# A later routing chain and spread lower parts in the first expert mixture

## The chip, the cores and the metric

The kernel runs on one core of one Trainium2 chip. The metric is the device time of one execution in microseconds. Three executions of the kernel before took 829.95, 829.97 and 831.6 us; the median is 829.97 us.

A core has five engines that run side by side, each through a queue of its own in order: TensorE (PE in the profile; its weight loads are PEld), VectorE (DVE), ScalarE (ACT), GpSimd (POOL) and SyncE (SP), which issues the plain DMAs. They wait for each other on semaphores only.

## The reference

Three stages follow one another. The first is a linear-attention recurrence with complex decay over 4 batches, 8 heads, 768 steps and 48 channels; its result is 3072 tokens of 384 values. The second is a mixture of experts with a fixed capacity:

```python
logits = x @ w_gate                      # 3072 x 8
order = np.argsort(-logits.flatten())
for idx in order:                        # best pairs first
    tok, e = int(idx) // E, int(idx) % E
    if assigned[tok] >= 0 or counts[e] >= cap: continue
    assigned[tok] = e; counts[e] += 1    # cap = 3072 / 8 = 384
for e in range(E):
    mask = assigned == e
    out[mask] = np.maximum(x[mask] @ w1[e], 0.0) @ w2[e]   # 384 -> 1024 -> 384
```

Every expert gets exactly 384 tokens, but which ones depends on all the others. The third stage is a mixture without capacity: a token whose score is positive goes to its best expert, the result is scaled by a softmax weight and added to the token; all other tokens pass unchanged.

## The kernel before

The attention takes the first 298 us of the profiled execution. The change starts behind it, in `moe1` (line 1230), the capacity mixture; the last mixture (`moe2_round`, line 1323) follows it.

**Routing.** `route` (line 794) finds, in round p, the expert that fills up next and its 384 tokens. It looks for the threshold of the scores in four digits of six bits each. One digit is: 0/1 rows `R` on DVE (line 833), twelve products `hist` on PE that count them (line 849), `need` and `junk` on DVE (lines 854, 855), one small product `ce` on PE (line 859), `bp` on DVE (line 861), and then `A`, `C` and `R` of the next digit. After the fourth digit DVE makes `es` (line 885, the expert's number), `MT` (its members), and the keys of the next round (`prelude`, line 214: `lgm`, `best`, `eq`, `kx`, `dg` and so on). `slots` (line 902) turns the members into row numbers: two products `pp`, a chain on DVE that ends in `L` (line 939) and `R2` (line 931), twelve products `pi` (line 944), and on DVE `odd`, `x` and `ids` (lines 949 to 956). The round of expert p + 1 runs during the products of expert p.

**Products.** Every float32 product is made of three: each operand is split into a high part (`hi`, ACT, line 980) and a lower part (`lo` = raw - hi, line 981), and high by high, high by low and low by high are added (PASSES). Layer 1 (line 1022) has 8 half blocks of 9 products `psh` each; after each, ACT makes the high part of `hT` (line 1035) and DVE the lower part (line 1036), and two PSUM tiles take turns, so the products of half block f + 2 wait for the lower part of f. Layer 2 (line 1068) has 72 products `psy`. The gathered rows `xg` of the next expert are transposed (`pst`, line 1018) inside layer 2 and split into `xT` (lines 989, 990). `ffn1_out` (line 1100) and `route2` (line 1115) then send an expert's result to the last mixture: products `px` and `pp`, some thirty small DVE operations, and six indirect DMAs on POOL (line 116).

**Weights.** An expert has eight tiles of raw weights (`weights`, line 967), four for each layer, in four buffers: a load into a buffer waits until the lower part has read what was there. `fetch_w` (line 992) loads the first four as soon as `es` is known. `fetch_x` (line 1002) issues three indirect DMAs on POOL that gather `xg`, and the other four loads.

**What sets the order.** `layer1` and `layer2` call `tick` (line 1240) twice per half block: 16 times in layer 1 and 16 in layer 2. A routing generator that yields the number n goes on n ticks later; COUNT, SUMS, NEXT, RANKS and ROWS (line 60) are these numbers, for round 0, 1, 2 and so on. PE's order in this stage is the order of the code, held by added dependencies (`pe`, line 100). On the other engines a scheduler decides at build time; once built, each queue is fixed.

## Time and profile before

| what | value |
|---|---|
| median of three executions | 829.97 us |
| the profiled execution's own time | 835.9 us |
| its span, first to last instruction | 834.1 us |
| attention | 0 to about 298 us |
| routing of the first expert and wait for its rows | 298 to 332.5 us |
| experts 0 to 5 of the capacity mixture | 332.5 to 597.3 us |
| expert 6, with no routing left | 597.3 to 626.7 us |
| expert 7 and the last mixture | 626.7 to 834.1 us |

An expert is counted from its first `psh` product to the next expert's first. "Busy" of an engine is the union of its instructions in a stretch. "idle before" is the time for which an engine stood still in front of an instruction, and behind the arrow stands what released it. PEclk is the granted share of TensorE's full clock: 1.00 is 2.4 GHz, 0.50 is 1.2 GHz.

### The profile page before, as it was taken

The numbers are of one execution on the slowest core, as the hardware profiler recorded it, in microseconds if no ns is written. First come the engines' busy times: TensorE is split into PE (matmuls) and PEld (weight loads), VectorE is DVE, ScalarE is ACT, GpSimd is POOL, SyncE is SP. The second block draws the span as 40 slices with busy tenths as digits, with TensorE's granted clock in tenths as the row PEclk, the third lists the DMA queues.
The fourth block names the chain that finished last, engine by engine and source line by source line (L and its number), as shares of the span: only waits on it lengthen the run. The fifth ranks groups of instructions, "written<-read, shape, count | busy, mean of one in ns | idle before, by whom it ended". The sixth has DMA issues, their size and how long they took to land.

```text
span 834.1 us, 14172 instructions
## 1 busy us (share of the span) xinstructions
PE 700.2 (84%) x5162; PEld 642.7 (77%) x5162; DVE 529.6 (63%) x1438; ACT 389.9 (47%) x680; POOL 266.5 (32%) x190
## 2 busy tenths in 40 slices
PE   1578879889999952888888979698899989999992
PEld 1468778778989942677777869598799888999992
DVE  8859779788746557766667676858434455454450
ACT  5775678677745303135242332324323445455540
POOL 1000544634511002010404031313322467677750
PEclk9669899999999975889898999999899999999997
DMA  9996354643211005233333232326402466566620
GB/s 192 222 263 130 67 129 105 138 96 81 54 39 39 20 29 180 72 109 94 108 102 96 84 116 92 117 74 205 141 30 63 137 208 217 177 208 219 225 97 12
DMA packets 183775, 99.80 MB, mean 120 GB/s; under 512 B 130899, under 2 KB 180937, under 8 KB 183696
## 3 DMA queue, kind: packets, MB, share of 16 engines
q1 hardware_dynamic: 178000, 86.79, 38.7%
q0 software_dynamic: 5696, 12.02, 4.3%
q8 instruction: 42, 0.69, 0.3%
q14 instruction: 37, 0.30, 0.1%
HBM read 82.03 MB, written 22.27 MB: 125 GB/s over the span
## 4 chain that ended last, share of the span: by engine, by line
PE 42%; DVE 17%; DMA 15%; issue 9%; ACT 9%; POOL 4%; SPq 1%; POOLq 0%; DVEq 0%; ACTq 0%
PE psy L109 11%; DMA raw<-in_moe_w_dram 11%; PE psh L109 8%; DVE lo L981 4%; PE py L109 4%; PE pa L109 3%; PE pt L112 3%; PE f L436 3%; PE hist L109 3%; PE px L109 3%; ACT hi L980 2%; PE st L109 2%; DVE hT L1036 1%; PE pst L112 1%; DMA xs<-x,ix 1%
## 5 line engine op out<-in xcount | busy, mean ns | idle before, releaser
L109 PE MATMUL psh<-xT,hi 128*128 128x384 f32 (+1 forms) x720 | 142.5, 330 | 21.4 <-DVE hT L1036 19.8
L980 ACT CAST hi<-raw 128x768 fp32r<-128x768 f32 x128 | 106.7, 835 | 104.3 <-DMA raw<-in_moe_w_dram 81.2
L109 PEld LDWEIGHTS psh<-xT,hi 128*128 128x128 f32 x720 | 116.6, 194 | 27.8 <-DVE hT L1036 24.2
L109 PE MATMUL psy<-hT,hi 128*128 128x384 f32 x384 | 105.4, 357 | 0.0
L981 DVE TENSOR_TENSOR lo<-raw,hi 128x768 fp32r<-128x768 f32 x82 | 86.0, 1067 | 30.5 <-ACT hi L980 30.2
L981 POOL TENSOR_TENSOR lo<-raw,hi 128x768 fp32r<-128x768 f32 x46 | 85.1, 1871 | 29.2 <-ACT hi L980 28.7
L116 POOL DMA_INDIRECT xs<-x,ix x24 | 28.0, 1167 | 199.5 <-issue 109.1
L1036 DVE SCALAR_TENSOR_TENSOR hT<-psh,hT 128x384 fp32r<-128x384 f32 (+1 forms) x120 | 59.1, 499 | 45.8 <-ACT hT L1035 44.8
L1035 ACT ACTIVATE hT<-psh 128x384 fp32r<-128x384 f32 (+1 forms) x120 | 53.1, 446 | 73.9 <-PE psh L109 69.4
L109 PE MATMUL psh<-xT,lo 128*128 128x384 f32 (+1 forms) x360 | 76.2, 320 | 0.0
L109 PE MATMUL psy<-hi,hT 128*128 128x384 f32 x272 | 74.9, 346 | 0.0
L109 PEld LDWEIGHTS psy<-hT,hi 128*128 128x128 f32 x384 | 72.8, 200 | 1.1 <-issue 0.2
L109 PE MATMUL psy<-hT,lo 128*128 128x384 f32 x192 | 69.8, 364 | 0.0
L989 ACT CAST xT<-pst 128x384 fp32r<-128x384 f32 (+1 forms) x47 | 19.0, 442 | 101.5 <-PE pst L112 101.5
L109 PEld LDWEIGHTS psh<-xT,lo 128*128 128x128 f32 x360 | 61.0, 193 | 0.0
L109 PE MATMUL pa<-qT,kT 96*128 96x128 f32 x384 | 52.9, 284 | 1.7 <-ACT kT L501 1.7
L109 PEld LDWEIGHTS pa<-qT,kT 96*128 96x128 f32 x384 | 49.2, 200 | 2.5 <-ACT kT L501 1.8
L1006 POOL DMA_INDIRECT xg<-xd,ids x24 | 26.5, 1104 | 75.6 <-PE ce L109 41.5
L109 PEld LDWEIGHTS psy<-hi,hT 128*128 128x128 f32 x272 | 49.0, 192 | 0.0
L990 DVE TENSOR_TENSOR xT<-pst,xT 128x384 fp32r<-128x384 f32 (+1 forms) x47 | 22.3, 499 | 39.6 <-ACT xT L989 39.5
L109 PE MATMUL px<-iw,yT 128*128 128x104 f32 (+1 forms) x336 | 45.7, 281 | 0.7 <-ACT yT L552 0.7
L109 PE MATMUL psy<-lo,hT 128*128 128x384 f32 x136 | 46.0, 338 | 0.0
(342 smaller groups left out, 1478.9 us busy)
## 6 DMA issues: line engine op xcount, KB each, us to landing
raw<-in_moe_w_dram SPq DMA_DIRECT2D x128, 384.0 KB, 4.0
xs<-zt SPq DMA_DIRECT2D x8, 579.0 KB, 7.0
re<-in_a_re_dram SPq DMA_DIRECT2D x24, 192.0 KB, 3.7
im<-in_a_im_dram SPq DMA_DIRECT2D x24, 192.0 KB, 3.7
q<-in_q_dram SPq DMA_DIRECT2D x24, 192.0 KB, 3.6
k<-in_k_dram SPq DMA_DIRECT2D x24, 192.0 KB, 3.8
vp<-in_v_dram SPq DMA_DIRECT2D x24, 192.0 KB, 3.3
xd<-xo SPq DMA_DIRECT2D x24, 192.0 KB, 1.9
```

The source lines that it names most:

```text
L109: return pe(nc.tensor.matmul(*a, **kw))
L112: return pe(nc.tensor.transpose(*a))
L116: st = nc.gpsimd.indirect_dma_start(out=dst, out_offset=bass.IndirectOffsetOnAxis(ap=idx, axis=0), in_=src, in_offset=None, bounds_check=b ...
L436: nc.tensor.matmul(f, lhsT=m, rhs=x, start=(j == 0), stop=(j == len(mm) - 1))
L980: nc.scalar.copy(out=hi, in_=raw)
L981: st = (V if g in shared else nc.gpsimd).tensor_tensor(out=lo, in0=raw, in1=hi.bitcast(F32), op=ALU.subtract)
L989: nc.scalar.copy(out=xT[0][:, c, :], in_=ps)
L990: V.tensor_tensor(out=xT[1][:, c, :], in0=ps, in1=xT[0][:, c, :].bitcast(F32), op=ALU.subtract)
L1006: st = nc.gpsimd.indirect_dma_start(out=xg[:, j, :], out_offset=None, in_=xd, in_offset=bass.IndirectOffsetOnAxis(ap=ids[:, j:j + 1], axis=0))
L1035: nc.scalar.activation(out=hT[0][:, f, :], in_=ps, func=ACTF.Relu)
L1036: V.scalar_tensor_tensor(out=hT[1][:, f, :], in0=ps, scalar=0.0, in1=hT[0][:, f, :].bitcast(F32), op0=ALU.max, op1=ALU.subtract)
```

## The change

The numbers that set the ticks change. A pause REST of 5 ticks comes between the end of a round and the next round's keys; COUNT goes from 14 to 16 and then 10, RANKS from 4 to 2, ROWS from 8 to 5, and the transposes go from tick 11 to tick 13 of layer 2. Weight tiles beyond the first four are no longer fetched when the rows are, but one at a time; their lower parts are put in a list, `lows`, and every third tick takes one from it. For round 1 the first three digits have one-tick pauses, and they run, with the transposes of expert 0's rows, in seven ticks ahead of expert 0's first product. The instructions and their number on each engine stay the same, and so does the order on SP and POOL.

```diff
-    COUNT, SUMS, NEXT, RANKS, ROWS = (1, 14), (1, 3), (1, 2), (3, 2, 4), (10, 10, 8)
-    START, TURN, AHEAD = 4, 11, 4
+    REST, COUNT, NEXT, SUMS, RANKS, ROWS = 5, (16, 10), 2, 3, 2, 5
+    START = 7
+    TURN, AHEAD, LOW = 13, 4, 3
...
-        def pause(v):
-            return 1 if p == 0 else v[min(p, len(v)) - 1]
+        def pause(v, soon=False):
+            return 1 if p == 0 or soon else v
...
-                yield pause(SUMS if r else COUNT)
+                yield pause(SUMS if r else COUNT[min(max(p, 2) - 2, 1)], p == 1 and r + 1 < nd)
...
-                yield pause(NEXT)
+                yield pause(NEXT, p == 1 and r + 1 < nd)
...
             parts.append(slots())
+            yield pause(REST)
+    lows = []
+    def lower(stop=0):
+        while len(lows) > stop:
+            lows.pop(0)()
-    def weights(s1_, s2_, shared=(), hook={}):
+    def weights(s1_, s2_, shared=(), hook={}, later=False):
...
-        def more(stop, after=None):
-            for g in range(len(res), stop):
+        def more(stop=None):
+            stop = len(res) + 1 if stop is None else stop
+            for g in range(len(res), min(stop, 2 * NG)):
+                if later:
+                    lower(3)
...
-                if after is not None:
-                    tc.add_manual_dep(st.ins, after.name, order, reason="rows first")
...
+                def low(g=g, raw=raw, hi=hi, both=both):
+                    lo = ws.tile([128, KD * FG * 128], F32R, tag="lo", name="lo")
...
+                if later:
+                    lows.append(low)
+                else:
+                    low()
...
-        return more(2 * NG, st.ins), xg
+        return xg
+    def turn1_steps(xg):
...
+        for j in range(3):
+            for c in range(KD):
+                tp(ps[c][:, j * 128:(j + 1) * 128], xg[:, j, c * 128:(c + 1) * 128], ident)
+            yield
+        for c in range(KD):
+            xsplit(ps[c], c, xT)
+        yield xT
...
+            n_[0] += 1
+            if not force:
+                if n_[0] % LOW == 0:
+                    lower(max(0, len(lows) - 1))
+                    for p in sorted(more):
+                        if len(lows) < AHEAD:
+                            more[p]()
...
-        (w1h, w2h), xg = got[0]
-        for _ in range(START):
+        turn[:] = [None, True]
+        first_rows = turn1_steps(got[0])
+        for i in range(START):
             tick()
-        xT = turn1(xg, True)
-        turn[1] = True
+            if i in (3, 5, 6):
+                next(first_rows)
+            if i in (2, 4):
+                lower(len(lows) - 1)
+        for xT in first_rows:
+            pass
+        lower()
         last = None
         for p in range(E):
+            more[p](AHEAD)
+            while len(more[p](0)[0][-1]) < 2:
+                lower(len(lows) - 1)
...
+            hT = layer1(more[p](0)[0], xT, CAP, tick, last)
+            w2h = more[p](2 * NG)[1]
+            while len(w2h[-1]) < 2:
+                lower(len(lows) - 1)
```

The scheduler makes of this, on DVE, three places that the prediction speaks of. The first is the wait for expert 0's rows, from `best` of round 1's keys on (in each piece, `lo` is a lower part of the weights and `ids` are the row numbers). Before:

```order
L222 TENSOR_REDUCE best_497<-lgm 128x24
L233 TENSOR_TENSOR eq_500<-lgm,best_497 128x192
L236 TENSOR_TENSOR eq_500<-eq_500,rev 128x192
L954 TENSOR_SCALAR x_2929<-pi 32x3 x4
L238 TENSOR_REDUCE m_498<-eq_500 128x24
L956 CAST ids<-x_2929 128x3
```

The same place on DVE in the changed kernel, from the instruction behind `best` on:

```order
L1000 TENSOR_TENSOR lo<-raw,hi 128x768
L237 TENSOR_TENSOR eq_500<-lgm,best_497 128x192
L958 TENSOR_SCALAR x_2929<-pi 32x3 x4
L1000 TENSOR_TENSOR lo<-raw,hi 128x768
L240 TENSOR_TENSOR eq_500<-eq_500,rev 128x192
L960 CAST ids<-x_2929 128x3
```

Two lower parts now stand ahead of `ids`. The second place is DVE at the end of layer 1 of expert 2 (and likewise of 1, 3 and 4), where `slots` ends in `L` and `R` (the code's R2), for which the `pi` products wait. Before:

```order
L928 TENSOR_TENSOR oh<-i_450,sh__4535 128x288
L939 TENSOR_TENSOR L_4543<-i_450,sl__4536 128x384 x2
L1151 TENSOR_TENSOR rk<-pp_4577,base_494 128x24
L931 TENSOR_TENSOR R_4541<-oh,pos 128x288
L1036 SCALAR_TENSOR_TENSOR hT<-psh,hT 128x384
```

The same place on DVE in the changed kernel:

```order
L932 TENSOR_TENSOR oh<-i_450,sh__4592 128x288
L943 TENSOR_TENSOR L_4600<-i_450,sl__4593 128x384 x2
L241 TENSOR_SCALAR dg_501<-dg_501 128x96
L1000 TENSOR_TENSOR lo<-raw,hi 128x768
L242 TENSOR_REDUCE m_498<-eq_500 128x24
L1066 SCALAR_TENSOR_TENSOR hT<-psh,hT 128x384
L935 TENSOR_TENSOR R_4598<-oh,pos 128x288
```

A lower part, a reduction and the eighth `hT` (of layer 1's last half block) now stand between `L` and `R`; on PE, 22 products stand between `pp` and `pi`, where 36 stood. The third place is DVE from the results of `pi` to the row numbers `ids` and on to `need` of the next round's first digit. Before:

```order
L949 TENSOR_SCALAR odd<-pi 32x12
L952 TENSOR_TENSOR x_2929<-pi,odd 32x3 x4
L1036 SCALAR_TENSOR_TENSOR hT<-psh,hT 128x384
L956 CAST ids<-x_2929 128x3
L981 TENSOR_TENSOR lo<-raw,hi 128x768 x4
L854 TENSOR_SCALAR need<-hist 8x64
```

The same place on DVE in the changed kernel:

```order
L953 TENSOR_SCALAR odd<-pi 32x12
L848 SCALAR_TENSOR_TENSOR PT<-fx,dt__4642 128x48
L1000 TENSOR_TENSOR lo<-raw,hi 128x768
L250 TENSOR_TENSOR oh_481<-rev,ecode_496 128x24x8
L956 TENSOR_TENSOR x_2929<-pi,odd 32x3 x4
L1000 TENSOR_TENSOR lo<-raw,hi 128x768
L960 CAST ids<-x_2929 128x3
L1000 TENSOR_TENSOR lo<-raw,hi 128x768
```

Two lower parts now stand between `odd` and `ids`, and the four that stood together ahead of `need` are spread; five more stand between `dg` of the second piece and `odd`, so that all eight of an expert lie from the last half block of layer 1 to this `need`.

## Rows read from the trace of the kernel before

**Rows 1.** The page: engine totals, then the TensorE clock in 40 slices

```profile
PE 700.2 (84%) x5162; PEld 642.7 (77%) x5162; DVE 529.6 (63%) x1438; ACT 389.9 (47%) x680; POOL 266.5 (32%) x190
...
PEclk9669899999999975889898999999899999999997
```

**Rows 2.** Windows, one per expert 0 to 6: start:end, length, busy us (instructions)

```profile
332.50:380.90 48.40, 40.74 (x247) 35.76 (x247) 34.54 (x124) 13.14 (x23) 3.32 (x3) 0.83 0.25 78
380.90:424.90 44.00, 38.56 (x248) 34.25 (x248) 30.71 (x123) 15.58 (x28) 10.01 (x9) 0.92 0.32 100
424.90:469.80 44.90, 39.37 (x259) 34.86 (x258) 29.80 (x121) 14.74 (x28) 9.69 (x9) 0.92 0.31 97
...
512.80:556.50 43.70, 37.26 (x248) 32.67 (x246) 29.82 (x120) 14.00 (x27) 10.06 (x9) 0.96 0.32 100
556.50:597.30 40.80, 34.33 (x212) 31.24 (x213) 27.51 (x103) 16.39 (x29) 12.29 (x11) 0.92 0.54 167
597.30:626.70 29.40, 29.00 (x182) 28.18 (x181) 13.11 (x40) 11.71 (x24) 7.24 (x8) 1.00 0.20 66
```

**Rows 3.** Waits of PE, experts 2 to 4: us in total, times, longest

```profile
PE psh L109 <- DVE hT L1036: 10.2, 7, 2.4
PE ce L109 <- DVE junk L855: 6.5, 3, 2.4
```

**Rows 4.** Windows behind waits: length, busy PE, PEld, DVE, ACT, POOL, PEclk

```profile
437.50:440.90 3.40, 3.40 (x12) 3.40 (x12) 3.40 (x10) 2.12 (x3) 0.00 (x0) 0.50 0.50 165
588.00:594.50 6.50, 5.20 (x22) 4.26 (x23) 2.52 (x9) 2.21 (x4) 0.00 (x0) 0.50 0.15 49
```

**Rows 5.** Timeline of PE, undisturbed products and what stands between them

```profile
420.28 0.34 PE L109 MATMUL psy<-hT,lo 128*128 128x384 f32 x1
420.55 0.85 PE L109 MATMUL hist<-R,oh 128*40 128x128 bf16 x12
421.32 0.62 PE L109 MATMUL psy<-hT,hi 128*128 128x384 f32 x2
...
628.24 1.20 PE L109 MATMUL psh<-xT,hi 128*128 128x384 f32 x6
...
629.80 2.27 PE L109 MATMUL px<-iw,yT 128*128 128x137 f32 x18
631.82 0.60 PE L109 MATMUL psh<-xT,hi 128*128 128x384 f32 x2
```

**Rows 6.** Windows of DVE from the last digit's bp to ids: length, busy; four experts' sum

```profile
428.60:449.70 21.10, 17.97 (x84) 0.92 0.48 152
...
sum 80.30, DVE 70.82; mean DVE 17.71
```

**Rows 7.** Timeline: lower parts in a row, and a split of a half block

```profile
448.91 0.56 DVE L1036 SCALAR_TENSOR_TENSOR hT<-psh,hT 128x384 fp32r<-128x384 f32 x1
449.45 3.56 DVE L981 TENSOR_TENSOR lo<-raw,hi 128x768 fp32r<-128x768 f32 x4
```

**Rows 8.** Timeline of row numbers, gathers and transposes, experts 0 and 5

```profile
366.37 0.17 DVE L956 CAST ids<-x 128x3 int32<-128x3 f32 x1
...
367.30 0.95 POOL L1006 DMA_INDIRECT xg<-xd,ids  x1 [41.54 <-PE ce L109]
...
584.44 0.99 POOL L1006 DMA_INDIRECT xg<-xd,ids  x1 [0.30 <-issue]
...
587.01 0.95 POOL L1006 DMA_INDIRECT xg<-xd,ids  x1 [0.30 <-issue]
588.04 0.47 PE L112 MATMUL pst<-ident,xg 128*128 128x128 f32 x1 [2.91 <-DMA xg<-xd,ids]
...
590.25 1.75 PE L112 MATMUL pst<-ident,xg 128*128 128x128 f32 x7 [0.66 <-DMA xg<-xd,ids]
```

**Rows 9.** Timeline of the wait for expert 0's rows

```profile
318.93 0.16 DVE L956 CAST ids<-x 128x3 int32<-128x3 f32 x1
...
319.02 0.83 ACT L980 CAST hi<-raw 128x768 fp32r<-128x768 f32 x1 [0.32 <-DMA raw<-in_moe_w_dram]
...
319.29 1.82 DVE L981 TENSOR_TENSOR lo<-raw,hi 128x768 fp32r<-128x768 f32 x2
320.04 2.32 POOL L1006 DMA_INDIRECT xg<-xd,ids  x1 [20.86 <-DMA raw<-in_moe_w_dram]
...
332.51 1.01 PE L109 MATMUL psh<-xT,hi 128*128 128x384 f32 x2
```

**Rows 10.** Timeline of DVE: one digit follows another with nothing else to do

```profile
304.98 0.22 DVE L854 TENSOR_SCALAR need<-hist 8x64 f32<-8x64 f32 x1 [1.01 <-PE hist L109]
...
308.36 0.21 DVE L854 TENSOR_SCALAR need<-hist 8x64 f32<-8x64 f32 x1 [1.01 <-PE hist L109]
```

## Prediction: what the change will do to the time

> **What bounds the kernel now.** I read the engine totals first, then one window per expert, then PE's waits inside those windows, and then the timeline around the two longest kinds. In the totals the reader is to see that PE is busy for 84% of the span and DVE for 63% [rows 1], so a DVE that is late costs time only where PE stands behind it. The windows show where that is. Expert 6, which has no routing beside it, takes 29.4 us; experts 1 to 4 take 44.0, 44.9, 43.0 (from 469.8 to 512.8) and 43.7, a mean of 43.9, with DVE busy for about 30 of them [rows 2]. The 14.5 us between are the routing. Its own products explain little: a `hist` between two `psy` moves the second from 420.28 + 0.17 to 421.32, which is 0.87 us [rows 5], and four of them are 3.5. PE's waits are the larger part: over experts 2 to 4, 10.2 us for `hT` and 6.5 us for `junk` ahead of `ce` [rows 3], 5.6 us per expert. Behind such waits PE's clock falls: it stood at 0.50, its level of 1.2 GHz, from 437.5 to 440.9 and, behind the waits for expert 6's rows, from 588.0 to 594.5 [rows 4]. Each microsecond of products there costs half a microsecond. So the stage is bound by DVE's queue in order: lower parts, round ends and keys stand ahead of what PE needs next.
>
> The profiled execution took 835.9 us by its own time, 5.9 over the median 829.97; 1.8 of it lies outside the span. I work out differences in its span and put them on the median, since a difference of some microseconds scales by under 1%.
>
> **The change part by part.** No instruction is added or taken away; only where DVE, ACT and PE meet is moved. So the question is what is late next. I follow one of experts 1 to 4 in the changed order.
>
> *Layer 1's waits.* DVE no longer has lower parts of the next expert ahead of the splits of half blocks 0 to 6; what stands between two splits there is digits and `route2`. PE's 10.2 us for `hT` over three experts, 3.4 each, should shrink to some tenths, and the 6.5 us at `ce`, 2.2 each, go too, since the four lower parts ahead of `need` (3.56 us [rows 7]) no longer stand together. Taken alone that is 5.6 us per expert, plus up to 1.7 for each 3.4 us at the lower clock.
>
> *What is late next.* The last digit now ends in half block 5, and from there everything up to `ids` has to pass DVE: round end, the tail of `route2`, the next keys, `slots`, three splits and seven lower parts. I price this run from the same run before. There DVE was busy for 17.7 us on the mean of four experts [rows 6]. By a count of the two orders the new run has four splits fewer (about 0.5 each [rows 7]), 17 small operations fewer (an estimate of 0.1 each from 17.7 us over some 82 instructions, the large ones taken off) and three lower parts more (0.89 each, a quarter of 3.56 [rows 7]): 17.7 - 2.0 - 1.7 + 2.7 = 16.7. With 0.5 for waits on `pp`, I take 17.2 us. Its other bound is the wall time before, 80.3 / 4 = 20.1 us [rows 6].
>
> Two waits follow. On PE 22 products (3.8 us) stand between `pp` and `pi`, while on DVE two splits, a lower part and some twenty operations of keys and `slots` stand between `scan` and `R`, by the share of the run an estimate of 6.5 us: PE waits about 3 us at `pi`. Then `ids` come late. From `ids` to the first gather it is 0.93 us, from the first gather to the third 2.57, and from the third's start to the transposes that wait for it 3.24 [rows 8]: 6.7 us. The transposes stand 45 products behind the second `pi`, which PE passes in less, so it waits there too.
>
> *The loop.* A chain that closes over an expert sets the period then. `ids` to landed rows 6.7; the last seven transposes 0.9 (1.75 at half clock [rows 8]); 13 products at 0.173 (nine take 629.80 - 628.24 [rows 5]) 2.25; one `hist` 0.87; layer 1 up to the fourth digit's `ce`: 50 products 8.65, two `hist` 1.74, `px` 2.02 (to the next product's start [rows 5]), and 1.0 for the small products and short waits, 13.4; the DVE run 17.2. The sum is 41.3 us. The lower clock behind the wait at `pi` is covered, since PE would wait for the rows anyway. Behind the wait for rows it is not: 3.4 to 6.5 us at half speed [rows 4] cost 1.7 to 3.2, where they come at all. I take 1.5, which gives 42.8 against 43.9: -1.1 per expert, -4.4 for four. Unseen, the loop may lie between 40 (the run as short as 16, no fall of the clock) and 46 (20.1 and a fall).
>
> *The wait for expert 0's rows.* Two lower parts now stand ahead of `ids`, and the second needs a cast that starts at 319.02 and takes 0.83 [rows 9]. So `ids`, at 318.93 before, come near 322, and the rows 3 us later. Behind the eight lower parts and the keys the first digit's `need` comes near 332.5. A digit takes 308.36 - 304.98 = 3.38 us [rows 10]; three of them, the fourth's `R` and three splits end near 342.5, where layer 1 began at 332.5 [rows 9]. That costs 10 us. What it gives back: layer 1 of expert 0 loses three digits and their waits. It is now 72 products 12.5, one `hist` and small ones 2.4, about 2 for the clock that is still low at first, and 3 for the same wait at `pi`: 20 us, to 362.5. Layer 2 is 12.5 + 3.5 for two `hist`, one `ce` and transposes, to 378.0 where 380.9 was [rows 2]. I take -3, between -6 and +4; its rows come early enough for expert 1.
>
> *Expert 5.* It carries the same late run without the next keys. Its six scatters on POOL still stand ahead of the gather, so rows come about as late as DVE lets them; the waits before its transposes, 2.91 for the first rows and 0.66 for the third [rows 8], shrink to about 2. I take -1.3, between -4 and +2. Experts 6 and 7 and the last mixture keep their order but for a later transpose that has 13 products (2.25 us) as cover: nothing; if that cover failed, 0.5 us.
>
> The sum is -3 - 4.4 - 1.3 = -8.7: 829.97 - 8.7 = 821 us.
>
> *A rule against it.* The first gather of expert 0 ran beside two lower parts and took 2.32 us on POOL [rows 9]; beside no lower part it took 0.99 [rows 8]. The Trainium skill says in "GPSIMD Engine Reference", 1. Specifications, that GpSimd shares its SBUF interfaces with VectorE and contends with DVE instructions that have two SBUF inputs, as a lower part has. By that rule, the trace agrees, the gather that now runs right beside the last lower part of an expert starts its transfers later.
>
> **The rivals.** *DVE no longer binds.* If the run were short enough that one of the two waits goes, an expert would take some 39.3 us: 4 x 4.6 + 4.3 = 22.7 less, 807 us. PE's own work, 29.4 for an expert without routing [rows 2] and 3.5 for `hist`, is far enough below, and DVE's 30 busy microseconds would fit; against it, the run is a chain in one queue, and the rows behind it go through POOL and DMA. Chance 0.22.
>
> *The rows decide, and later (slower).* The place is the transposes in layer 2 of experts 1 to 4. If the run takes 20.1 us, as before on the wall, because lower parts in it wait for their loads, the loop is 41.3 + 2.9 + 1.7 = 45.9: +2.0 per expert, +8, with nothing won in experts 0 and 5: 838 us. It decides from a run of about 18.5 us on, where the loop passes the present period. For it: the four buffers tie each load to a lower part. Against: a load and a cast need about as long as the DVE work between a lower part and the fourth behind it. Chance 0.20.
>
> *Gathers beside lower parts.* If each gather is longer by the 1.33 us seen between 2.32 and 0.99 [rows 8, 9], and the second by half of it, the loop grows by 2.0 and four experts by 8: 829 us. The rule named above is this one. Chance 0.10.
>
> *It does not do what it says.* The lower parts are to go one per three ticks, but the built order has all eight of an expert within some 22 rows of DVE. If bunching moves the waits one for one, the time stays at 830. For it: the two sums of waits, about 7 new against 5.6 and the clock, are close. Chance 0.13.
>
> **How the numbers follow.** Forecast 0.35, with its own range 814 to 828. The measurement tells about 0.2%, 1.7 us, from no change. Faster: 0.31 of the forecast, the first rival 0.22, and 0.04 of the last two: 0.57. Same: 0.04 of the forecast, 0.05 of the gathers, 0.05 of the last: 0.14. Slower: 0.20 for late rows, 0.09 for the others' upper ends: 0.29. The range reaches to both main rivals: 805 to 838.
>
> **What would show it.** In the new profile `hT` should go as PE's main releaser in layer 1, and `ce` with it; two new waits should stand once per expert in layer 2, `pi` for DVE's `R` of about 3 us and `pst` for the rows of 2 to 4 us. Expert 0's first `psh` should start near 342. DVE should run without a gap from the fourth `bp` to `ids`, for about 17 us. If `pst` does not wait, the first rival holds; if it waits over 6 us, the second. The forecast is wrong if experts 1 to 4 come out below 41 or above 45 us.

## The result: 0.5% slower, and the profile after

Twenty executions of each kernel: median 834.29 us (827.93 to 841.83) against 829.03 (825.15 to 833.55), ratio 1.0052 with a 95% interval of 1.0028 to 1.0076. The forecast was 821 us, faster; the time lies inside the range, on the other side of no change. A ratio here and below leaves out executions more than 1.5% above the fastest of their kernel, so it is not always that of the medians, and the changed kernel's first trace is of such an execution, the longest of the twenty (841.83 us). What follows from it is therefore held against a second trace further on.

The page of the changed kernel answers to [rows 1]: the totals hardly move.

```profile
PE 703.3 (84%) x5162; PEld 647.0 (77%) x5162; DVE 532.4 (63%) x1438; ACT 394.1 (47%) x680; POOL 278.9 (33%) x190
```

Its windows, one per expert 0 to 6 and then the rest, with the columns of [rows 2]:

```profile
342.30:379.40 37.10, 34.47 (x205) 31.46 (x206) 25.82 (x87) 12.91 (x23) 3.06 (x3) 0.90 0.32 102
379.40:423.20 43.80, 38.76 (x248) 34.53 (x248) 29.95 (x120) 16.24 (x28) 12.99 (x9) 0.92 0.32 100
423.20:467.40 44.20, 39.05 (x247) 34.95 (x246) 30.29 (x120) 14.87 (x27) 12.24 (x9) 0.88 0.31 99
467.40:508.70 41.30, 37.37 (x248) 33.49 (x247) 30.15 (x120) 14.73 (x27) 11.32 (x9) 0.92 0.34 106
508.70:553.40 44.70, 37.24 (x249) 32.86 (x248) 30.23 (x120) 15.10 (x27) 14.98 (x9) 0.92 0.31 98
553.40:598.60 45.20, 38.51 (x239) 34.05 (x238) 31.15 (x121) 17.46 (x30) 15.84 (x12) 0.85 0.46 149
598.60:628.10 29.50, 29.02 (x182) 28.18 (x181) 13.06 (x40) 11.68 (x23) 6.33 (x7) 1.00 0.21 68
628.10:840.10 212.00, 188.10 (x1250) 183.61 (x1249) 93.04 (x217) 92.30 (x180) 114.96 (x75) 0.95 0.47 154
```

Experts 1 to 4 take 174.0 us together where 175.6 stood, expert 5 is 4.4 us longer than in [rows 2], and from expert 7 on it takes 212.0 us where 834.1 - 626.7 = 207.4 stood. PE's waits in experts 2 to 4, against [rows 3]: `hT` and `ce` are gone, two others have their place.

```profile
PE pi L113 <- DVE R L935: 9.9, 3, 3.7
PE pst L116 <- DMA xg<-xd,ids: 6.3, 6, 3.0
```

With 0.3 at `ce` that is 16.5 us of waits, against 16.7 in [rows 3] and 0.9 more there at `pp`. Expert 4 shows the loop in pieces. PE first, then DVE, then POOL, timeline rows with the idle time ahead of each in brackets:

```profile
531.13 0.36 PE L113 MATMUL pi<-R,L 128*64 128x24 f16 x6 [2.64 <-DVE R L935]
...
545.53 0.47 PE L116 MATMUL pst<-ident,xg 128*128 128x128 f32 x1 [3.00 <-DMA xg<-xd,ids]
...
548.00 1.76 PE L116 MATMUL pst<-ident,xg 128*128 128x128 f32 x7 [0.74 <-DMA xg<-xd,ids]
```

```profile
522.46 0.15 DVE L865 TENSOR_REDUCE bp<-ce 128x1 f32<-128x8 f32 x1
...
530.17 0.55 DVE L1066 SCALAR_TENSOR_TENSOR hT<-psh,hT 128x384 fp32r<-128x384 f32 x1
530.63 0.45 DVE L935 TENSOR_TENSOR R<-oh,pos 128x288 f16<-128x288 f32 x1
...
533.06 0.95 DVE L1000 TENSOR_TENSOR lo<-raw,hi 128x768 fp32r<-128x768 f32 x1
...
539.62 0.16 DVE L960 CAST ids<-x 128x3 int32<-128x3 f32 x1
```

```profile
533.16 3.68 POOL L120 DMA_INDIRECT xs<-x,ix  x1 [0.30 <-DVE m L248]
...
542.16 1.25 POOL L1027 DMA_INDIRECT xg<-xd,ids  x1 [0.31 <-DVE C L844]
```

From the start at 508.70 to the fourth `bp` it takes 13.8 us (forecast 13.4); to `ids` 17.2 (17.2); from `ids` to the transposes of the third rows 8.4 (6.7), because the gather starts 2.5 us behind `ids` and not 0.93, held on POOL by scatters that grew beside lower parts; and on to the next expert, at 553.40, 5.4 (4.0, and 1.5 for the clock), with the seven transposes at half clock, 1.76 us. The sum is 44.7, against 41.3 and, with the clock, 42.8. Expert 4 of the second trace, below, has 13.7, 18.0, 7.1 and 5.5; there the gather starts 1.2 us behind `ids`.

### The profile page after: what moved, and what is told of

Its sections match the earlier page's. It is cut to its first block, busy times and chain, and to the rows that moved or that the text cites. A ratio compares the mean times of both kernels' runs of the same rounds, so it can differ in the third digit from the quotient of the medians.

```text
span 840.1 us, 14188 instructions
## 1 busy us (share of the span) xinstructions
PE 703.3 (84%) x5162; PEld 647.0 (77%) x5162; DVE 532.4 (63%) x1438; ACT 394.1 (47%) x680; POOL 278.9 (33%) x190
## 5 line engine op out<-in xcount | busy, mean ns | idle before, releaser
L1000 DVE TENSOR_TENSOR lo<-raw,hi 128x768 fp32r<-128x768 f32 x82 | 92.1, 1126 | 32.4 <-ACT hi L994 32.2
L113 PE MATMUL psy<-hT,hi 128*128 128x384 f32 x384 | 107.3, 362 | 0.0
L120 POOL DMA_INDIRECT xs<-x,ix x24 | 38.2, 1593 | 184.3 <-issue 100.0
L113 PEld LDWEIGHTS psy<-hT,hi 128*128 128x128 f32 x384 | 75.4, 206 | 0.8
L1027 POOL DMA_INDIRECT xg<-xd,ids x24 | 26.2, 1092 | 80.7 <-DVE ids L960 39.6
L1011 DVE TENSOR_TENSOR xT<-pst,xT 128x384 fp32r<-128x384 f32 (+1 forms) x47 | 22.7, 500 | 44.9 <-ACT xT L1010 44.3
L113 PE MATMUL px<-iw,yT 128*128 128x104 f32 (+1 forms) x336 | 47.8, 289 | 1.6 <-DVE xo L565 0.9
L113 PEld LDWEIGHTS px<-iw,yT 128*128 128x128 f32 x336 | 42.8, 197 | 5.5 <-issue 3.7
```

The source lines that it names most:

```text
L113: return pe(nc.tensor.matmul(*a, **kw))
L120: st = nc.gpsimd.indirect_dma_start(out=dst, out_offset=bass.IndirectOffsetOnAxis(ap=idx, axis=0), in_=src, in_offset=None, bounds_check=b ...
L1000: (V if later or g in shared else nc.gpsimd).tensor_tensor(out=lo, in0=raw, in1=hi.bitcast(F32), op=ALU.subtract)
L1011: V.tensor_tensor(out=xT[1][:, c, :], in0=ps, in1=xT[0][:, c, :].bitcast(F32), op=ALU.subtract)
L1027: nc.gpsimd.indirect_dma_start(out=xg[:, j, :], out_offset=None, in_=xd, in_offset=bass.IndirectOffsetOnAxis(ap=ids[:, j:j + 1], axis=0))
```

## The experiments

Every kernel is an edit of the changed one unless another is named, and is timed against the kernel before. That one's medians beside them were 829.8 to 831.8 us, so medians of two runs compare to about 2 us. A stage's time comes from one trace of a kernel.

**Second traces.** `again` is the changed kernel, `before_again` the kernel before, both unedited.

> The changed kernel once more, unedited, for a second trace of it. Theory 1 (the loop): experts 1 to 5 of the first mixture are set by the chain from the fourth digit's bp over the row numbers and the gathered rows to the transposes, and what the change lost lies there: experts 1 to 4 again about 43.5 us, expert 5 again about 45 where it was 40.8, and behind expert 6 the time of before, so that the 4.6 us that the first trace lost behind expert 6 are gone and the total is 3 to 5 us above before. Theory 2 (the tail): the change costs in the last mixture, whose instructions stand in the same order: expert 6's start is within 1 us of before and the 4 to 5 us behind it come again.

> The kernel before once more, unedited, for a second trace. It tells how far two traces of one program differ in each stage. Theory 1 (the loop): the stretch from the first hist to expert 6, 302.4 us in the first trace, comes out within 3 us of that, and the tail from expert 7's first product to the end, 207.5, within 1 us. Theory 2 (the tail): the same, and then the tail of the changed kernel, 212.0 and 210.8 in its two traces, is longer by more than two traces of one program differ. If the tail comes out near 210, what stands behind expert 7 tells the kernels apart no longer.

`again`: 834.12 us, ratio 1.0061 (1.0019 to 1.0104). `before_again`: 827.55 in its one run. Experts 1 to 4 in one window each, in the order before, before_again, changed, again (one fence per trace):

```profile
380.90:556.50 175.60, 152.62 (x998) 134.96 (x997) 120.38 (x486) 57.76 (x106) 39.98 (x36) 0.94 0.32 100
```

```profile
373.30:545.60 172.30, 149.44 (x998) 131.90 (x997) 120.38 (x486) 58.05 (x106) 40.10 (x36) 0.96 0.33 102
```

```profile
379.40:553.40 174.00, 152.42 (x986) 135.84 (x986) 120.62 (x480) 60.94 (x106) 51.53 (x36) 0.91 0.32 101
```

```profile
374.10:547.40 173.30, 151.70 (x987) 134.89 (x986) 120.31 (x480) 60.80 (x106) 54.76 (x36) 0.93 0.33 101
```

On the mean 43.5 us per expert before and 43.4 after. The granted clock (PEclk) is lower by 0.03 in both pairs, and POOL is busy for some 13 us more. Expert 5: 40.8 and 43.0 before, 45.2 and 43.5 after. The stretches from the first `hist` to expert 6, and from expert 7 to the end, in `before_again` and then in `again`:

```profile
291.80:588.60 296.80, 238.66 (x1589) 210.43 (x1589) 206.56 (x812) 95.96 (x169) 59.07 (x54) 0.89 0.35 109
618.00:825.80 207.80, 185.57 (x1251) 181.14 (x1249) 92.17 (x217) 92.63 (x180) 114.97 (x75) 0.96 0.49 157
```

```profile
291.80:590.90 299.10, 239.65 (x1590) 212.39 (x1590) 207.31 (x812) 99.54 (x169) 75.69 (x54) 0.87 0.34 107
620.40:831.20 210.80, 186.73 (x1250) 182.19 (x1249) 93.64 (x217) 92.14 (x180) 115.37 (x75) 0.95 0.48 155
```

The first stretch took 302.4 us in the kernel before's first trace, so two traces of it differ by 5.6 us, nearly twice what theory 1 allowed; the second differs by 0.4. A third trace of the changed order is at hand: `after_tail`, below, has the same instructions in the same order on every engine up to expert 6. Its first stretch, with 169.2 us for experts 1 to 4 and 44.9 for expert 5:

```profile
294.40:590.30 295.90, 238.03 (x1590) 210.92 (x1589) 207.41 (x812) 99.51 (x169) 75.15 (x55) 0.88 0.35 108
```

So the changed order took 302.7, 299.1 and 295.9 us there, the old one 302.4 and 296.8: the first mixture as a whole cannot be told from unchanged. What both traces show beyond their spread is the 3.0 to 4.6 us behind expert 7, which is theory 2.

**One part undone at a time.**

`start4` undoes the digits in the wait for expert 0's rows:

```diff
-    START = 7
+    START = 4
...
-            if i in (3, 5, 6):
-                next(first_rows)
-            if i in (2, 4):
-                lower(len(lows) - 1)
```

> One part undone: only the START ticks as before (4) run in the wait for expert 0's rows, and the rows are transposed behind them, so that expert 0's layer 1 starts earlier and carries three digits of round 2 more; the later routing ticks and the paced lower parts stay. If the ten us spent in that wait are not given back (theory 3, the start), this kernel is 3 to 8 us faster than the changed one, about 828. If the start is worth what the traces show, 1.5 us won (theory 1), expert 0's first psh comes near 333 and expert 1's near 381, and the kernel is 1 to 2 us slower than the changed one, 835 to 836.

840.59 us, 1.0165 (1.0093 to 1.0236): 6 us slower than the changed kernel, more than expected. START moves every round: with three digits left over, each fourth `bp` comes 17.2 us into an expert, and PE waits 31.2 us for rows in experts 1 to 5 (12.7 in the changed kernel's first trace):

```profile
PE pst L116 <- DMA xg<-xd,ids: 31.2, 15, 5.0
```

`ticks_old` undoes the ticks; a list holds the numbers of rounds 1, 2 and from 3 on:

```diff
-    REST, COUNT, NEXT, SUMS, RANKS, ROWS = 5, (16, 10), 2, 3, 2, 5
+    REST, COUNT, NEXT, SUMS, RANKS, ROWS = 0, (14, 14), 2, 3, (2, 2, 4), (5, 10, 8)
-    TURN, AHEAD, LOW = 13, 4, 3
+    TURN, AHEAD, LOW = 11, 4, 3
```

> One part undone: from round 2 on the routing has the ticks of before (COUNT 14, ROWS 10 and then 8, RANKS 4, no rest between rounds), and the transposes stand at tick 11; the digits in the wait for expert 0's rows and the paced lower parts stay. Theory 1 (the loop): the row numbers come earlier again in an expert, the two new waits (pi and pst) go, expert 5 returns to about 41, and since the lower parts no longer stand together, the waits for hT and ce stay below those of before: experts 1 to 4 about 43, in all 3 to 7 us faster than the changed kernel, 827 to 831. If the paced lower parts are what costs (theory 4), nothing changes: within 2 us of the changed kernel.

843.77 us, 1.0214 (1.0156 to 1.0273): slower by 10, against both theories. With the old ticks the paced lower parts meet the digits and splits of layer 1; the waits for `hT` are back, with `pp` beside them, in experts 1 to 5:

```profile
PE psh L113 <- DVE hT L1066: 16.1, 9, 3.0
PE pst L116 <- DMA xg<-xd,ids: 7.3, 6, 3.6
PE pp L113 <- DVE ohb L1162: 7.2, 4, 3.0
```

`lo_old` undoes the pacing:

```diff
-                if later:
-                    lows.append(low)
-                else:
-                    low()
+                low()
...
-                if n_[0] % LOW == 0:
-                    lower(max(0, len(lows) - 1))
...
+                more[want[0]](2 * NG)
```

> One part undone: weights are loaded and lowered as before, four tiles when the expert is known and four behind the gathers, none of them paced; the later routing ticks and the digits in the wait for expert 0's rows stay. Theory 1 (the loop): the DVE run from the fourth bp to the row numbers loses about four of its seven lower parts, 17.2 - 3.6 = 13.6 us; the loop shrinks by up to 3.6 us per expert, of which 2 come back as waits for hT or ce behind lower parts that stand together: 4 to 8 us faster than the changed kernel, about 828. Theory 4 (the pace): the same or better, experts 1 to 4 near 41 and the total near 822. If the pacing is what holds the changed kernel (its lower parts placed well), it is slower, 840.

825.58 us, 0.9973 (0.9933 to 1.0012): 8.5 us faster than the changed kernel, between theory 1 (828) and theory 4 (822); the DVE run is 14.0 to 15.5 us. So the pacing costs. What the late routing and the digits in the wait gain without it is not clear of nothing, since the interval includes 1. The parts do not add up: undone one by one, two cost 6.5 and 9.7 us and the third wins 8.5.

**The wait for rows.**

`turn15` has one new number:

```diff
-    TURN, AHEAD, LOW = 13, 4, 3
+    TURN, AHEAD, LOW = 15, 4, 3
```

> One number of the changed kernel: TURN 15 for 13, so that the transposes of the next expert's rows stand nine products (1.6 us) later. Theory 1 (the loop): the wait for rows, 2.1, 1.5, 0.3 and 4.5 us in experts 1 to 4 and 4.4 in expert 5, loses up to 1.6 each, but the split of the rows then stands closer to layer 1, which has 0.8 us of products as cover: experts 1 to 4 near 43, 828 to 834. If the missing cover costs more than the wait, layer 1 begins with a wait for xT of 1 to 2 us: 836 to 840.

`rows7` has another:

```diff
-    REST, COUNT, NEXT, SUMS, RANKS, ROWS = 5, (16, 10), 2, 3, 2, 5
+    REST, COUNT, NEXT, SUMS, RANKS, ROWS = 5, (16, 10), 2, 3, 2, 7
```

> One number of the changed kernel: ROWS 7 for 5, so that the pi products stand nine products later on PE. Theory 1 (the loop): PE no longer waits for R at pi, but the row numbers hang on DVE and come when they came, so the wait moves to the transposes: experts 1 to 4 between 42.5 and 44, the kernel within 3 us of the changed one, 831 to 837. If the wait at pi and the fall of the clock behind it are a price of their own (theory 5, two waits): about 2.6 and 1.7 us go per expert, 813 to 820.

`turn15`: 821.94 us, 0.9856 (0.9815 to 0.9896), 12 us faster than the changed kernel by one number and better than any theory had it. Waits of PE in experts 1 to 5 of `again` and of `turn15`:

```profile
PE pi L113 <- DVE R L935: 14.4, 5, 3.7
PE pst L116 <- DMA xg<-xd,ids: 11.9, 10, 2.1
```

```profile
PE pi L113 <- DVE R L935: 15.1, 5, 3.7
PE pst L116 <- DMA xg<-xd,ids: 2.2, 2, 1.6
```

9.7 us of waiting went, and experts 1 to 5 fell from 216.8 to 203.1, 13.7. The rest, 4.0, fits the clock: these experts ran for 34 us at half clock in `again` and for 27 in `turn15`, by the granted clock, and half of the difference is 3.4. The missing cover before layer 1 cost nothing that shows. `rows7`: 832.01, 1.0023 (0.9989 to 1.0057); `pi` fell from 14.4 to 6.5 and `pst` rose from 11.9 to 14.8, with 5.9 new at `hist`: the wait moved, as theory 1 said. Theory 5 falls.

**What makes the rows late.**

`lo_late` holds the paced lower parts until the row numbers are made:

```diff
+                    if later and started[0]:
+                        tc.add_manual_dep(st.ins, ids_of[0].name, order, reason="rows first")
-                if n_[0] % LOW == 0:
+                if want[0] is None if started[0] else n_[0] % LOW == 0:
```

> One edit to the changed kernel: the lower parts of experts 1 to 7 are held back until the row numbers of the next expert are made, and then go one per tick. Theory 1 (the loop): the DVE run from the fourth bp to the row numbers loses its seven lower parts, 17.2 - 6.2 = 11 us, the wait for the rows goes and the wait at pi shrinks from 3 to about 1: experts 1 to 4 near 40, the kernel 12 to 20 us faster than the changed one, 815 to 822. Theory 4 (the pace): what costs is that loads and lower parts of the next expert come late; holding them back further makes layer 1 or layer 2 of the next expert wait for weights: slower than the changed kernel, 838 or more.

`lo_gather` is `lo_old` with the first four lower parts too put behind the gathers:

```diff
-                low()
+                if later and gather[0] is None and started[0]:
+                    lows.append(low)
+                else:
+                    low()
...
+                lower()
                 more[want[0]](2 * NG)
```

> The kernel with unpaced lower parts (lo_old, 825.6), and in it the first four lower parts too stand behind the gathers of the row numbers, all eight then in a row. Theory 1 (the loop): the DVE run, 14.0 to 15.5 in lo_old, falls to 11 or 12, the wait at pi by about 1.5, and the wait for rows goes: 1 to 2 us per expert, 818 to 822. A rival, the digits: the lower parts in a row stand ahead of need of the next round's first digit, and the wait at ce that the change removed comes back, 2 to 4 us per expert: 826 to 836.

Both came out as theory 1 had it. `lo_late`: 821.47 us, 0.9882 (0.9839 to 0.9926). `lo_gather`: 818.27, 0.9753 (0.9696 to 0.9810); its seven executions lie between 808.9 and 823.5. The DVE run fell to 11 to 14 and 11 to 12 us, the period of experts 1 to 4 to 40.7 and 40.1, not the 37 that a loop six microseconds shorter would give. Expert 4 of `lo_gather` on DVE and then on POOL shows what now holds the gathers:

```profile
509.59 0.16 DVE L865 TENSOR_REDUCE bp<-ce 128x1 f32<-128x8 f32 x1
...
521.06 0.17 DVE L960 CAST ids<-x 128x3 int32<-128x3 f32 x1
```

```profile
523.25 1.43 POOL L120 DMA_INDIRECT out_dram<-x,io  x1 [0.30 <-DVE lo L1000]
524.99 0.99 POOL L1029 DMA_INDIRECT xg<-xd,ids  x1 [0.30 <-issue]
```

`ids` are there at 521.06, but POOL is at its scatters until 524.7: the chain has passed from DVE to POOL's queue. It hardly holds PE, though, which waits 2.6 us for the rows over experts 1 to 4 and 9.4 at `pi`. What makes up the rest of the 40.1 was not tested.

`after_out` puts the three output scatters (`rest`) of an expert behind the next gathers; `fetch_x` calls what is in `outs`. Those of expert 5 are left out of the computation, in `go_turn15_out` below too.

```diff
+        if p + 2 < E:
+            outs.append(rest)
+        else:
+            rest()
...
+        while outs:
+            outs.pop(0)(st.ins)
```

> One edit to the changed kernel: of the six scatters of an expert the three into the output go behind the gathers of the next rows on POOL, for experts 0 to 5. Theory 6 (POOL's queue): the row numbers are there 0.3 to 2 us before the first gather starts, which waits on POOL behind the sixth scatter in experts 1, 4 and 5; the gathers start at once, and in expert 5 by 2 us earlier: the wait for rows loses about 1 us in experts 1 and 4 and 2 in expert 5, the kernel is 3 to 6 us faster than the changed one, 828 to 831. Theory 1 (the loop) alone, with DVE as what decides: 832 to 835. If the scatters behind the gathers make their landing slower, 836 or more.

841.89 us, 1.0127 (1.0069 to 1.0186). The gathers did start about 1 us behind `ids`, but the built order on DVE moved too, and its run grew to 18 to 20 us in experts 1 to 4. As a test of POOL alone it is inconclusive; as an edit it loses.

**The wait at `pi`.** `lo_rest` is `lo_old` with numbers that were to make the keys later:

```diff
-    REST, COUNT, NEXT, SUMS, RANKS, ROWS = 5, (16, 10), 2, 3, 2, 5
+    REST, COUNT, NEXT, SUMS, RANKS, ROWS = 9, (12, 6), 2, 3, 2, 5
```

> The kernel with unpaced lower parts (lo_old, 825.6), and in it the rest between two rounds goes from 5 to 9 ticks and the pause before the first digit from 16 and 10 to 12 and 6, so that the next keys come four ticks later on DVE and the products of the digits stay where they are. Theory 1 (the loop): the keys leave the stretch between scan and R, the wait at pi, 2.6 to 4.0 us in lo_old, falls below 1.5, the row numbers come some 2 us earlier, and the kernel is 4 to 10 us faster than lo_old, 816 to 822. If the wait at pi is not worth time since PE would wait for the rows instead, nothing changes: 824 to 827. If the keys then come too late for the first digit, ce or hist waits and the kernel is slower, 830.

`go_rows7` is `lo_gather` with the edit of `rows7`, `go_rows7_turn14` with that and

```diff
-    TURN, AHEAD, LOW = 13, 4, 3
+    TURN, AHEAD, LOW = 14, 4, 3
```

> The fastest kernel so far (lo_gather, 818.3: unpaced lower parts, all behind the gathers) with ROWS 7 for 5. There the DVE run is 11 us and the rows come in time, so that the wait at pi, 1.8 to 3.1 us, is PE's largest. Theory 1 (the loop): with the run that short the loop no longer closes, what binds is PE's own work and this wait; the wait goes, 1 us of it comes back at the transposes: experts 1 to 4 from 40.1 to about 38.5, 810 to 815. If the rows take all of it back: 816 to 820.

> As go_rows7, and TURN 14 for 13. Theory 1: what came back at the transposes goes as well, with one tick of cover left for the split: 0 to 1 us per expert below go_rows7, 806 to 813. If the split of the rows then comes late for layer 1, slower than go_rows7 by 1 us per expert: 815 to 820.

`lo_rest`: 825.34 us, 0.9961 (0.9928 to 0.9995), as `lo_old`; the wait at `pi` stayed, 14.6 us in experts 1 to 5 against 15.0. That says nothing about the keys, though: in the built order of `lo_rest` they stand on DVE between the fourth `bp` and `R` just as in `lo_old`, so the edit did not move them, and whether they make `R` late was not tested. In the DVE rows of expert 4 above `R` stands right behind the last split `hT` of layer 1, and a lower part stands between `L` and that split. In `lo_gather`, where that lower part comes later, `pi` waits 1.77 us in expert 4 where it waited 2.64. `go_rows7`: 828.80, 0.9991 (0.9960 to 1.0023), ten microseconds slower than `lo_gather`, against theory 1. In experts 1 to 5 the wait at `pi` fell from 12.2 to 3.0 us and that at `pst` rose from 5.6 to 20.4: the rows, whose gathers start 3.9 to 4.8 us behind `ids` on POOL, took back more than all. `go_rows7_turn14`: 823.21, 0.9920 (0.9886 to 0.9954), in between.

**The gains together, and the stretch behind expert 7.**

`go_turn15` is `lo_gather` with the edit of `turn15`; `go_turn15_out` adds that of `after_out`. `after_tail` is the changed kernel with three casts of the last mixture's first expert held back on ACT (`behind` is its last `xT` cast):

```diff
-                nc.scalar.copy(out=hi, in_=raw)
+                st = nc.scalar.copy(out=hi, in_=raw)
+                if behind[0] is not None:
+                    tc.add_manual_dep(st.ins, behind[0].name, order, reason="rows first")
```

> The two edits that helped, together: the lower parts unpaced and behind the gathers (lo_gather, 818.3), and TURN 15 for 13 (turn15, 821.9). Both shorten the wait at the transposes. Theory 1 (the loop): what is left of that wait in lo_gather, 0.5, 0.3, 1.9, 0.2 and 2.9 us in experts 1 to 5, goes, and PE's own work and the wait at pi bind: 3 to 5 us below lo_gather, 813 to 816. If the two gains are the same gain, 817 to 820.

> As go_turn15, with the three scatters into the output behind the gathers as in after_out. Theory 6 (POOL's queue): in lo_gather the row numbers are made at 25 us of an expert and the first gather starts at 29, behind the sixth scatter; with TURN 15 the rows come in time anyway in experts 1 to 4, so that the gathers' earlier start is worth something in expert 5 alone: 1 to 2 us below go_turn15. If nothing waits for the gathers any more: the same within 1.5 us. If the scatters then reach into the next expert's, slower by 1 to 3.

> One edit to the changed kernel, in the last mixture alone: on ACT three of the casts hi of its first expert's layer 2 weights, which stand between the casts xT of its rows and wait for their loads, go behind them. On every other engine the order of the first mixture stays, and the last mixture's but for two small swaps on DVE. In two traces of the changed kernel the stretch from expert 7 to the end is 212.0 and 210.8 us, in two of the kernel before 207.5 and 207.8, though the order is the same: these loads land 1 us later. Theory 2 (the tail): the late loads cost time through ACT's order; the three waits for xT at the start of the last mixture's layer 1, 2.1 us, and the fall of the clock behind them go: tail near 208, the kernel 2 to 4 us faster than the changed one, 830 to 832. If the tail is longer for another reason, nothing changes: 833 to 835.

`go_turn15`: 815.79 us, 0.9813 (0.9767 to 0.9860), by its ratio no faster than `lo_gather`. Its first `hist` to expert 6 took 277.7 us, 6.8 less than in `lo_gather`; second traces of these two orders, in the kernels below, have 278.6 and 290.0, so there the gains are two. But expert 6 took 31.4 and the rest 213.9. `go_turn15_out`: 821.74, 0.9891 (0.9840 to 0.9943), slower. `after_tail`: 832.67, 1.0017 (0.9983 to 1.0050).

What `after_tail` acts on, ACT in the last mixture's first expert, in `before_again` and in the changed kernel:

```profile
645.32 0.84 ACT L980 CAST hi<-raw 128x768 fp32r<-128x768 f32 x1 [2.58 <-DMA raw<-in_moe_w_dram]
646.06 0.37 ACT L989 CAST xT<-pst 128x256 fp32r<-128x256 f32 x1
```

```profile
656.03 0.83 ACT L994 CAST hi<-raw 128x768 fp32r<-128x768 f32 x1 [3.07 <-DMA raw<-in_moe_w_dram]
656.77 0.37 ACT L1010 CAST xT<-pst 128x256 fp32r<-128x256 f32 x1
657.76 0.83 ACT L994 CAST hi<-raw 128x768 fp32r<-128x768 f32 x1 [0.63 <-DMA raw<-in_moe_w_dram]
658.50 0.36 ACT L1010 CAST xT<-pst 128x256 fp32r<-128x256 f32 x1
```

and PE there in the changed kernel:

```profile
657.65 0.38 PE L113 MATMUL psh<-xT,hi 128*128 128x256 f32 x1 [0.54 <-DVE xT L1011]
658.92 0.39 PE L113 MATMUL psh<-xT,hi 128*128 128x256 f32 x1 [0.89 <-ACT xT L1010]
659.93 1.20 PE L113 MATMUL psh<-xT,hi 128*128 128x256 f32 x4 [0.62 <-ACT xT L1010]
```

The rows' casts stand in ACT's queue behind casts of weights. The four loads of these weights, issued at the same distance from expert 7, took this to land (KB each, median us), in `before_again` and in the changed kernel:

```profile
raw<-in_moe_w_dram SPq DMA_DIRECT2D x4, 384.0 KB, 4.8
```

```profile
raw<-in_moe_w_dram SPq DMA_DIRECT2D x4, 384.0 KB, 5.8
```

So the rows' casts, whose operands are there, come a microsecond late. In `after_tail` these waits went and that layer ended 2.6 us earlier than in `again`, but by the end it had all been given back in small pieces: 210.9 against 210.8. Other kernels speak against these loads as the cause of the longer stretch too. `ticks_old` has the order of the kernel before behind expert 7 on every engine; there the four loads land as late as in the changed kernel, and yet the stretch takes 209.3 us:

```profile
raw<-in_moe_w_dram SPq DMA_DIRECT2D x4, 384.0 KB, 5.9
```

In `lo_rest`, again with that order, they land after 4.8 us, and it takes 210.2. With this one order the stretch took 207.4 to 212.0 us over fourteen traces of twelve kernels.

`go_turn15_tail` and `lo_gather_tail` add the edit of `after_tail` to those two kernels.

> The fastest so far (go_turn15, 815.8) with the edit of after_tail: three casts hi of the last mixture's first layer 2 weights go behind the casts xT of its rows on ACT. In go_turn15 the stretch behind expert 7 is 213.9 us, with 2.3 us of waits for xT at its start and 6.8 us at half clock behind them. Theory 2 (the tail, through ACT's queue): these waits and the fall go, the tail is 209 to 211, the kernel 3 us faster, 811 to 814. If they are given back later, as in after_tail, whose tail stayed at 210.9 though its start came 2.6 us earlier: 814 to 817.

> lo_gather (818.3) with the same edit, where the tail was 209.6 us and its first layer 1 had no long wait for xT. Theory 2 (the tail, through ACT's queue): there was little to win, 0 to 1 us: 817 to 819. If the tail hangs on the fall of the clock somewhere else, the same. A tail near 208 as in the kernel before, and 816, would say that ACT's order is the whole difference.

`go_turn15_tail`: 808.93 us, 0.9739 (0.9699 to 0.9778), the fastest kernel here by its median; by the ratio it cannot be told from `lo_gather`. `lo_gather_tail`: 819.74, 0.9877 (0.9834 to 0.9921), no faster than `lo_gather`; its stretch behind expert 7 is 206.9, 2.7 shorter, but its first mixture, in the same order, came out longer, 290.0 against 284.5. In experts 1 to 5 of `go_turn15_tail` PE waits 12.2 us at `pi` and 0.3 at `pst`. Its two stretches:

```profile
293.90:572.50 278.60, 234.05 (x1590) 209.12 (x1589) 204.28 (x808) 97.17 (x166) 60.68 (x53) 0.88 0.34 113
603.90:810.10 206.20, 183.72 (x1250) 179.70 (x1249) 96.41 (x219) 92.34 (x181) 115.49 (x75) 0.97 0.49 158
```

With the casts moved the second stretch is 206.2 where it was 213.9. So ACT's queue does pass late loads on to PE at the start of that mixture: the waits for `xT` in its first layer 1 went in all three kernels. Over the whole stretch that came with 2.7 and 7.7 us in two kernels, one trace each, and with nothing lasting in the changed one. What makes the stretch longer in the changed kernel, and where `after_tail` gives its 2.6 us back, stays open.

## Why the forecast was wrong, point by point

What waits, and where, was forecast rightly. What failed are three of the four terms of the sum: experts 1 to 4, expert 5, and the last mixture, which was put at nothing. The differences are those of the means over two traces of each kernel.

- *What waits.* Right: `hT` and `ce` all but vanished, `pi` waits 2.6 to 3.7 us once per expert in 1 to 4, `pst` 0.3 to 4.5. Expert 0 began at 342.3, as said, partly by luck: from the first `hist` on it is 47.7 us in the forecast, 46.4 and 45.7 in the traces.
- *The DVE run.* Right: 16.7, 18.1, 16.7 and 17.2 us in experts 1 to 4, a mean of 17.2 (17.4 in the second trace), and the fourth `bp` near 14.
- *The wait for expert 0's rows, -3.* The working itself gives less: 362.5 + 12.5 + 3.5 is 378.5 and not 378.0, so -2.4. From the first `hist` to expert 1 it took 83.8 us before and 82.9 after: -0.9, inside its bounds, though the two traces of before alone are 4.6 apart.
- *Experts 1 to 4, -1.1 each.* This step failed in size: 43.5 to 43.4, -0.1 each (about -0.5 with the third trace of the changed order). The new waits took the place of the old ones, and what the forecast won was the small difference of two large numbers. The loop of 42.8 came out at 43.4, each term within about half a microsecond: 13.9 us to the fourth `bp` where I had 13.4, and 7.2 and 6.9 from `ids` to the last transposes where I had 6.7. The first gather, with scatters ahead of it on POOL here too, starts 1.0 to 1.2 us behind `ids` in seven of eight experts and 2.5 in expert 4 of the first trace, where I took 0.93. The rest is the base: I set the loop against 43.9 from one trace, while the second gave 43.1.
- *Expert 5, -1.3.* This step failed: 41.9 to 44.4, +2.5, beyond its bounds of -4 and +2 (44.9 in the third trace of the changed order). The wait for the rows, which was to shrink, stayed: 4.2 and 4.1 us before, 4.4 in both traces after. The row numbers came early enough, but the gathers ran beside four of expert 6's loads and took 4.7 to 6.8 us to land where those of the kernel before took 3.2 to 4.0. And PE's clock stood at 0.5 for longer, from 584.9, just behind the wait at `pi`, to 598.5, 13.6 us, and 10.2 in the second trace, where it had been 6.8 and 10.3. How much of the 2.5 us each of these makes was not tested.
- *Experts 6, 7 and the last mixture, 0.* This step failed: +3.8 behind expert 7. I put it at nothing by the order of instructions, which is indeed the same on every engine, and named the transposes as the one thing that could lose cover. What the traces show in its place is that the same order takes 207.4 to 212.0 us from kernel to kernel, so order alone does not fix it. Casts behind late loads make PE wait 2.1 us for `xT` there in both traces, where it waited 1.4 and 1.1, but moving them won nothing in this kernel. The cause of the +3.8 stays open.
- *The rivals.* "It does not do what it says", 830 us and a chance of 0.13, was nearest in what it says: waits moved about one for one, 29.5 us to 28.1 in experts 1 to 5 of the first pair and 30.1 to 27.7 of the second. "DVE no longer binds" gives 39.3 us for an expert without a working; kernels with a shorter run came near it, 40.1 in `lo_gather` and 39.6 in `go_turn15`, but not through DVE alone. "Gathers beside lower parts" was right on the neighbour and wrong on the victim: the gathers stayed at 1.09 us, the scatters ahead of them grew. POOL's rows of the scatters before and after:

```profile
L116 POOL DMA_INDIRECT xs<-x,ix x24 | 28.0, 1167 | 199.5 <-issue 109.1 <-ACT hT L1035 57.0 <-DVE ix L1162 32.5
```

```profile
L120 POOL DMA_INDIRECT xs<-x,ix x24 | 38.2, 1593 | 184.3 <-issue 100.0 <-ACT hT L1065 55.8 <-ACT hi L994 28.0
```

The rule of the Trainium skill in "GPSIMD Engine Reference", 1. Specifications, agrees with these rows: 1167 ns became 1593 when lower parts were spread over the scatters. The second traces have 1155 and 1557, and in `lo_gather`, whose lower parts stand behind the gathers, it is 1120.

The sum: -0.9 - 0.3 + 2.5 + 0.1 (expert 6) + 3.8 and 0.5 in the attention, which the change does not touch, make 5.7, the difference of the mean spans; -8.7 was forecast. That the time lies inside the range is luck: its upper part was there for a DVE run of 20.1 us, and the run was 17.2.

## What to carry to other kernels

Where a late chain is followed by a fixed place that consumes its result, moving other work off one wait mostly moves the wait to that place; look at the consumer's place first, since moving it by nine products was worth 12 us here. Judge a pace or an order by what it stands beside on every in-order queue, POOL's and ACT's too: lower parts beside scatters made scatters longer with gathers behind them, and casts behind loads made the rows' casts late. Whether that costs time in the end has to be measured. And take a base for small differences from two traces: one stretch differed by 5.6 us between two of the same kernel.

## What the hardware showed that was not expected

- An indirect scatter that takes 0.98 us on POOL took 3.68 beside lower parts on DVE, and 3.69 at the same place in the second trace.
- Loads in the same order, issued at the same distance from expert 7, had a median of 4.8 us to landing in one kernel and of 5.8 and 5.9 in two traces of the other.
- One order of instructions on all engines, behind expert 7, took 207.4 to 212.0 us in different kernels, but differed by 0.4 and 1.2 us between two traces of one kernel.
- The sum of PE's waits does not give the time. Two traces of the changed kernel had 1.4 and 2.4 us fewer waits in experts 1 to 5 than those of before, and these experts took 2.8 and 1.5 us longer, at a clock lower by 0.03 in experts 1 to 4. In `after_tail`, with the same order there, the clock stood at 0.95, and they took 214.2 us, less than in either trace of before (216.4 and 215.3).
